# Row-block loading of W1 and six-bank accumulation for the first two token tiles of a fused attention and MLP kernel

## The chip, the cores and the metric

The kernel runs on one core of a Trainium2 chip. The metric is device time in microseconds of one execution. Before the change it took 204.91 us, the median of three runs (204.8 to 204.93).

A core has five engines that run beside each other: TensorE (PE in the profile; its weight loads are listed apart as PEld), VectorE (DVE), ScalarE (ACT), GpSimd (POOL) and SyncE (SP, which here only issues DMAs). They meet through semaphores. Every engine works through its own list of instructions in order, so an instruction that waits holds up everything behind it on that engine.

## The reference

```
x  = A_x                                   # 1 x 2048 x 640, bf16
xn = (x - mean(x)) / sqrt(var(x) + 1e-5)   # layer norm, no scale
A  = linear_attention(xn, wqkv) @ wo       # 32 heads, phi(t) = where(t > 0, t + 1, exp(t)) + 1e-6
B  = gelu(xn @ w1 + b1) @ w2 + b2          # w1: 640 x 1536, w2: 1536 x 640
out = x + A + B
```

Only the layer norm and the first half of B, `gelu(xn @ w1 + b1)`, are touched.

## The kernel before, in words

The 2048 tokens are 16 tiles of 128. For each tile the kernel loads x (`x_in`, tokens on the partitions), computes the layer norm (`xn_tm`) and turns the result over, so that features lie on the partitions (`xnT`, five blocks of 128 features: `DT` = 5). With xnT the MLP's hidden activations are computed as 12 units (`JT` = 12), each of 128 hidden features: five matmuls, one for each block k of features, with a 128x128 piece of W1 as the weight and xnT as the moving operand, summed in a PSUM bank, followed by a Gelu on ScalarE that writes `HG`. Later stages compute k, v, q, the attention sums and the output; they aren't changed.

The program is written through a small planner. `Pl.ins(engine, fn, reads, writes)` appends an instruction to the list of that engine and works out which semaphores it must wait for. Nothing is reordered: the order of the calls is the order on each engine. There are eight PSUM banks, taken in a ring by `take`.

The layer norm of a tile has four steps: `ln_half` (L335) twice, each a `bn_stats` on half of the features on VectorE, the first followed by a small GpSimd add that puts the epsilon in; `ln_aggr` (L343), a `bn_aggr` on VectorE and then a power of -0.5 on GpSimd that gives `rstd`; and `ln_norm` (L356) on VectorE. The turn to xnT has two forms. For tiles 0, 1 and 2 TensorE transposes into PSUM (`transp`, L362, `transp_part`, L399) and VectorE or ScalarE copies the result to xnT. For tile 3 and later SyncE issues a DMA transpose (`xnT_dma`, L453).

The opening, in the order of the calls:

- SyncE loads x tile 0, x tile 1, then W1 in pieces of 512 columns, with x tiles 2 and later between and behind them. ScalarE's queue issues b1 and the first two row blocks of the first 512 columns (`r_W1A`).
- TensorE runs matmuls on zeros (`filler`) until x arrives.
- Tile 0 is normalised and turned in two parts (`norm_part`, `transp_part`), and `h_first` (L408) computes units 0 to 3 of tile 0, then of tile 1, with 128 columns a matmul, in one bank for each unit.
- `units(0, 2, 4, 12)` computes the other eight units for both tiles together, 256 columns a matmul, with the transpose of tile 2 put between units 8 and 9.
- `units(2, 1, 0, 10)` and `units(3, 1, 0, 10)` follow for tiles 2 and 3 alone, then the last two units of both, then tiles 4 and 5, and so on.

On VectorE the statistics and norms of tiles 2 and 3 stand in the same list as the copies that TensorE's transposes feed, and the norm of each later tile follows in a loop.

Of the kernel before, what the change touches and what calls it, by code (L numbers as in the profile page):

```python
# [7 lines left out]
P = 128  # L8
# [104 lines left out]
def bass_parallel_sum__linear_attn_block__dense_activation_gelu__prompt_kernel(  # L113
# [24 lines left out]
    with contextlib.ExitStack() as es:  # L138
# [59 lines left out]
        def take(n):  # L198
            b = ring[0]
            if n == 2 and b % 2:  # L200
                b += 1
            b %= 8
            ring[0] = (b + n) % 8
            return b

        def bank(b, lo=0, hi=512):
            return ps[:, b * 512 + lo: b * 512 + hi]
# [9 lines left out]
        r_xb = [R_("xb%d" % t) for t in range(NT)]  # L217
        r_xn = [R_("xn%d" % t) for t in range(NT)]
        r_xnT = [R_("xnT%d" % t) for t in range(NT)]
        NW1 = 3  # L220
        r_W1A = R_("W1_0A")
        r_W1 = [R_("W1_%d" % i) for i in range(NW1)]
        r_Wq, r_Wk, r_Wv, r_W2 = R_("Wq"), R_("Wk"), R_("Wv"), R_("W2")
        r_Wo = [R_("Wo%d" % i) for i in range(2)]
        r_oT = [R_("oT%d" % i) for i in range(2 * DT)]
# [36 lines left out]
        def dma_w(eng, dst, src, res):  # L262
            Pl.ins(eng, lambda e: e.dma_start(dst, src), writes=[res], dma=True)  # L263

        w1v = B_w1.rearrange("(k p) n -> p k n", p=P)
        wqv = A_wqkv.rearrange("(k p) n -> p k n", p=P)
        FW = F // NW1
        def dma_w1(i, eng="sync"):
            dma_w(eng, W1[:, :, i * FW:(i + 1) * FW], w1v[:, :, i * FW:(i + 1) * FW], r_W1[i])
        KA = 2  # L270
        dma_x(0, 1)
        dma_w("scalar", b1tmp[:], B_b1.rearrange("(a p) -> a p", p=P), r_b1tmp)
        dma_w("scalar", W1[:, 0:KA, 0:FW], w1v[:, 0:KA, 0:FW], r_W1A)
        dma_x(1, 1)
        dma_w("sync", W1[:, KA:DT, 0:FW], w1v[:, KA:DT, 0:FW], r_W1[0])
        dma_w1(1)
        dma_x(2, 1)
        dma_w1(2)
        dma_x(3, 1)
        dma_x(4, 2)  # L280
        dma_x(6, 2)
# [40 lines left out]
        def filler(n):  # L322
            b = take(1)
            Pl.ins("tensor", [lambda e: e.matmul(bank(b), warm[:, 0:P], warm[:], start=True, stop=True)
                              for _ in range(n)], reads=[r_warm], writes=[B_[b]])
# [9 lines left out]
        def ln_half(t, h):  # L335
            s = t % 4
            Pl.ins(v, lambda e: e.bn_stats(stats[:, s, 6 * h:6 * h + 6], x_in[:, t, h * HW:(h + 1) * HW]),  # L337
                   reads=[r_x[t]], writes=[r_stats[s][h]])
            if h == 0:
                Pl.ins(g, lambda e: e.tensor_single_scalar(stats[:, s, 2:3], stats[:, s, 2:3], D * EPS, ALU.add),  # L340
                       reads=[r_stats[s][0]], writes=[r_stats[s][0]])

        def ln_aggr(t):  # L343
            s = t % 4
            Pl.ins(v, lambda e: e.bn_aggr(aggr[:, s, :], stats[:, s, :]),
                   reads=r_stats[s], writes=[r_aggr[s]])
            Pl.ins(g, lambda e: e.tensor_tensor(out=rstd[:, s:s + 1], in0=aggr[:, s, 1:2],
                                                in1=mhalf[:], op=ALU.pow),
                   reads=[r_aggr[s], r_small], writes=[r_rstd[s]])

        def ln_stats(t):
            ln_half(t, 0)
            ln_half(t, 1)
            ln_aggr(t)

        def ln_norm(t):  # L356
            s = t % 4
            Pl.ins(v, lambda e: e.tensor_scalar(xn_tm[:, t, :], x_in[:, t, :], aggr[:, s, 0:1], rstd[:, s:s + 1],  # L358
                                                ALU.subtract, ALU.mult),
                   reads=[r_x[t], r_aggr[s], r_rstd[s]], writes=[r_xn[t]])  # L360
# [16 lines left out]
        def h_unit(t0, n, jb):  # L377
            b = take(1)
            w = n * P
            tok = slice(t0 * P, t0 * P + w)  # L380
            Pl.ins("tensor", [(lambda e, k=k: e.matmul(  # L381
                bank(b, 0, w), W1[:, k, jb * P:(jb + 1) * P], xnT[:, k, tok],
                start=(k == 0), stop=(k == DT - 1))) for k in range(DT)],
                reads=[r_W1[jb * P // FW]] + r_xnT[t0:t0 + n], writes=[B_[b]])
            Pl.ins("scalar", lambda e: e.activation(  # L385
                HG[:, jb, tok], bank(b, 0, w), ACT.Gelu_apprx_tanh, bias=b1c[:, jb:jb + 1]),
                reads=[B_[b], r_b1c], writes=[r_HG[t][jb] for t in range(t0, t0 + n)])


        CA = 2 * P  # L390
        r_xnA, r_xnB = R_("xn0A"), R_("xn0B")

        def norm_part(t, lo, hi, res):
            s = t % 4
            Pl.ins(v, lambda e: e.tensor_scalar(xn_tm[:, t, lo:hi], x_in[:, t, lo:hi], aggr[:, s, 0:1], rstd[:, s:s + 1],
                                                ALU.subtract, ALU.mult),
                   reads=[r_x[t], r_aggr[s], r_rstd[s]], writes=[res, r_xn[t]])

        def transp_part(t, k0, k1, res):  # L399
            b = take(1)  # L400
            pT = bank(b).bitcast(BF16)
            Pl.ins("tensor", [(lambda e, k=k: e.transpose(pT[:, (k - k0) * P:(k - k0 + 1) * P],
                                                          xn_tm[:, t, k * P:(k + 1) * P], ident[:]))
                              for k in range(k0, k1)],
                   reads=[res, r_ident], writes=[B_[b]])
            return xnT[:, k0:k1, t * P:(t + 1) * P], pT[:, 0:(k1 - k0) * P].rearrange("p (k q) -> p k q", k=k1 - k0), b

        def h_first(t, jbs, resA, between=None):  # L408
            bs = [take(1) for _ in jbs]
            tok = slice(t * P, (t + 1) * P)  # L410
            for (ks, res) in (((0, 1), resA), ((2, 3, 4), r_xnT[t])):
                for i, (jb, b) in enumerate(zip(jbs, bs)):
                    Pl.ins("tensor", [(lambda e, k=k, jb=jb, b=b: e.matmul(
                        bank(b, 0, P), W1[:, k, jb * P:(jb + 1) * P], xnT[:, k, tok],
                        start=(k == 0), stop=(k == DT - 1))) for k in ks],
                        reads=[r_W1A if res is resA else r_W1[jb * P // FW], res], writes=[B_[b]])
                    if between and res is not resA and i in between:
                        between[i]()
            for jb, b in zip(jbs, bs):
                Pl.ins("scalar", lambda e, jb=jb, b=b: e.activation(  # L420
                    HG[:, jb, tok], bank(b, 0, P), ACT.Gelu_apprx_tanh, bias=b1c[:, jb:jb + 1]),
                    reads=[B_[b], r_b1c], writes=[r_HG[t][jb]])

        r_xnTA, r_xnTA1 = R_("xnT0A"), R_("xnT1A")
        r_xnA1, r_xnB1 = R_("xn1A"), R_("xn1B")
        Pl.ins("scalar", lambda e: e.activation(b1c[:, 0:1], warm[:, 0:1], ACT.Gelu_apprx_tanh),
               reads=[r_warm], writes=[r_b1c])
        filler(6)
        b1_step()
        filler(3)  # L430
        ln_stats(0)
        ln_half(1, 0)
        ln_half(1, 1)
        norm_part(0, 0, CA, r_xnA)
        norm_part(0, CA, D, r_xnB)
        ln_aggr(1)
        dA, sA, bA = transp_part(0, 0, 2, r_xnA)
        filler(1)
        dB, sB, bB = transp_part(0, 2, DT, r_xnB)
        Pl.ins("scalar", lambda e: e.activation(dA, sA, ACT.Copy), reads=[B_[bA]], writes=[r_xnTA])  # L440
        Pl.ins(v, lambda e: e.tensor_copy(dB, sB), reads=[B_[bB]], writes=[r_xnT[0]])
        norm_part(1, 0, CA, r_xnA1)
        norm_part(1, CA, D, r_xnB1)

        def copy_part(k0, k1, res, dst):
            d, s, b = transp_part(1, k0, k1, res)
            Pl.ins(v, lambda e: e.tensor_copy(d, s), reads=[B_[b]], writes=[dst])

        h_first(0, [0, 1, 2, 3], r_xnTA, {1: lambda: copy_part(0, 2, r_xnA1, r_xnTA1),
                                          3: lambda: copy_part(2, DT, r_xnB1, r_xnT[1])})  # L450
        h_first(1, [0, 1, 2, 3], r_xnTA1)

        def xnT_dma(t):  # L453
            Pl.ins("sync", lambda e: e.dma_start_transpose(xnT[:, :, t * P:(t + 1) * P], xn_tm[:, t, :]),
# [1 line left out]

        late = Pl.records["sync"][x_done:]
        del Pl.records["sync"][x_done:]
        JQ = JT // NW1

        def units(t0, n, lo, hi):
            for jb in range(lo, hi):
                h_unit(t0, n, jb)

        def ln_next(t):
            if t + 1 < NT:
                ln_half(t + 1, 0)
            ln_norm(t)
            if t + 1 < NT:
                ln_half(t + 1, 1)  # L470
                ln_aggr(t + 1)

        units(0, 2, JQ, 2 * JQ + 1)
        ln_stats(2)
        ln_norm(2)
        ln_stats(3)
        xnT_copy(2, transp(2))
        units(0, 2, 2 * JQ + 1, JT)
        ln_next(3)
        xnT_dma(3)  # L480
        units(2, 1, 0, 10)
        units(3, 1, 0, 10)
# [353 lines left out]
```

## Time and profile before

| | us |
|---|---|
| median of three runs | 204.91 |
| the profiled execution, own time | 205.15 |
| span of the profile | 203.5 |
| TensorE matmuls busy (share of the span) | 199.4 (98%) |
| VectorE busy | 122.1 (60%) |
| ScalarE busy | 73.6 (36%) |
| GpSimd busy | 14.4 (7%) |

The span runs from the first to the last instruction of the profiled execution; its own time is 1.65 us longer. All moments below are microseconds from the start of the span. Of the span's 1153 recorded matmuls, those on zeros count as busy too, so the busy share doesn't tell when the real work begins.

In the chain of work that ended last, every step is followed back to what released it; in the listing in order of time the columns are the start, the length and what ran. In the timeline the columns are start, length, engine, line, operation, output and inputs, shape, count, and in brackets the idle time of the engine before it with what ended it. In the table of windows the columns are the stretch, its length, the busy time (and count) of PE, PEld, DVE, ACT and POOL, the granted TensorE clock, the mean busy share of the 16 DMA engines and GB/s.

### The profile page before, as it was taken

The page shows a single profiled execution, that of the slowest core. Times are in us where ns is not written, and L with a number is a line of the kernel's source. Part 1 is how long each engine was busy: PE and PEld are TensorE (multiplying, and loading weights), DVE is VectorE, ACT ScalarE, POOL GpSimd, SP SyncE. Part 2 cuts the span into 40 slices and gives each one's busy share as a digit, 9 for nine tenths or more (in the row PEclk, how much of TensorE's full clock was granted, in tenths as well). Part 3 has the DMA queues.
Part 4 walks back from the last instruction along what each step waited for, and adds up shares of the span by engine and source line. Part 5 has one row for each costly group of instructions (what it writes and reads, how often), then busy time and mean ns, then how long its engine had stood idle before and what let it go on. Part 6 is the DMA issues. An engine that isn't in the chain of part 4 may idle for free.

```text
span 203.5 us, 3162 instructions
## 1 busy us (share of the span) xinstructions
PE 199.4 (98%) x1153; PEld 106.7 (52%) x1170; DVE 122.1 (60%) x246; ACT 73.6 (36%) x144; POOL 14.4 (7%) x43
## 2 busy tenths in 40 slices
PE   7999999999999999999999999999999999999996
PEld 2789885444444444644456565444444444444444
DVE  4579855000005899999458899595794297348222
ACT  3589886666667555121233596200000000000000
POOL 3136534000000000000000000000000000000000
PEclk9999999999999999999999999999999999999999
DMA  5974996999901111000179934117266926851541
GB/s 154 360 263 98 123 191 120 240 348 221 323 8 29 26 26 26 3 0 0 35 178 373 160 64 98 55 22 161 31 122 195 144 52 115 153 120 31 164 117 52
DMA packets 52550, 25.45 MB, mean 125 GB/s; under 512 B 38119, under 2 KB 52535, under 8 KB 52535
## 3 DMA queue, kind: packets, MB, share of 16 engines
q1 hardware_dynamic: 48782, 23.80, 50.1%
q10 hardware_dynamic: 3752, 1.45, 4.2%
q8 instruction: 9, 0.15, 0.3%
q14 instruction: 7, 0.05, 0.1%
HBM read 12.72 MB, written 2.62 MB: 75 GB/s over the span
## 4 chain that ended last, share of the span: by engine, by line
PE 90%; DMA 5%; DVE 2%; SPq 1%; issue 1%; POOL 0%; DVEq 0%
PE ps L745 29%; PE ps L381 21%; PE ps L584 11%; PE ps L573 8%; PE ps L532 8%; PE ps L710 7%; DMA xPK<-in_A_x_dram 3%; PE ps L563 2%; PE ps L523 2%; DMA xnT<-xn_tm 1%; DVE stats L337 1%; PE ps L598 1%; PE ps L616 1%; SPq L263 0%; DVE xn_tm L358 0%
## 5 line engine op out<-in xcount | busy, mean ns | idle before, releaser
L381 PE MATMUL ps<-xnT,W 128*128 128x256 bf16 (+2 forms) x372 | 50.5, 296 | 0.3
L385 ACT ACTIVATE HG<-ps,b1c 128x256 bf16<-128x256 f32 (+2 forms) x75 | 37.4, 522 | 13.5 <-PE ps L381 11.7
L745 PE MATMUL ps<-HG,W 128*128 128x512 bf16 x188 | 41.9, 379 | 0.2
L381 PEld LDWEIGHTS ps<-xnT,W 128*128 128x128 bf16 x375 | 32.2, 98 | 17.9 <-DMA xnT<-xn_tm 0.3
L745 PEld LDWEIGHTS ps<-HG,W 128*128 128x128 bf16 x192 | 18.8, 98 | 22.6
L584 PE MATMUL ps<-xnT,Wqkv 128*128 128x512 bf16 x97 | 22.4, 379 | 0.2
L745 PE MATMUL ps<-PQ,Msb 128*128 128x512 bf16 x78 | 17.8, 379 | 0.1
L532 PE MATMUL ps<-Wqkv,xnT 128*128 128x512 bf16 x78 | 17.8, 379 | 0.1
L573 PE MATMUL ps<-xPK,xn_tm 128*128 128x512 bf16 x78 | 17.2, 379 | 0.1
L337 DVE BATCH_NORM_STATS2 stats<-xPK 128x6 f32<-128x320 bf16 x32 | 13.7, 468 | 5.7 <-DMA xPK<-in_A_x_dram 5.7
L584 PEld LDWEIGHTS ps<-xnT,Wqkv 128*128 128x128 bf16 x100 | 11.3, 118 | 8.7
L507 ACT ACTIVATE xn_tm<-ps 128x512 bf16<-128x512 f32 x20 | 11.9, 597 | 9.5 <-PE ps L584 8.9
L510 DVE SCALAR_TENSOR_TENSOR PQ<-ps,xn_tm 128x512 bf16<-128x512 f32 x20 | 13.8, 692 | 2.1
L507 ACT ACTIVATE ek<-ps 128x512 bf16<-128x512 f32 x20 | 11.8, 597 | 8.4 <-PE ps L532 6.4
L518 DVE CAST b2c<-out_l 128x5 f32<-128x5 bf16 x1 | 0.2, 172 | 23.2 <-DMA out_l<-b2bc 23.2
L649 DVE TENSOR_REDUCE den_sb<-xn_tm 128x128 f32<-128x512 f32 x4 | 4.1, 1037 | 16.1 <-DMA xn_tm<-xn_tm 16.1
L751 DVE SCALAR_TENSOR_TENSOR W<-ps,b2c,xnT 128x512 bf16<-128x512 f32 x16 | 11.3, 734 | 2.8 <-PE ps L745 2.4
L532 PEld LDWEIGHTS ps<-Wqkv,xnT 128*128 128x128 bf16 x80 | 7.8, 98 | 9.4
L745 PEld LDWEIGHTS ps<-PQ,Msb 128*128 128x128 bf16 x80 | 7.8, 98 | 9.4
L573 PEld LDWEIGHTS ps<-xPK,xn_tm 128*128 128x128 bf16 x80 | 7.8, 98 | 9.3
L633 DVE SCALAR_TENSOR_TENSOR xn_tm<-PQ,z_sb,xn_tm 128x512 f32<-128x512 bf16 x16 | 12.0, 749 | 0.4
L510 DVE SCALAR_TENSOR_TENSOR xPK<-ps,ek 128x512 bf16<-128x512 f32 x16 | 11.1, 692 | 1.7
(66 smaller groups left out, 151.3 us busy)
## 6 DMA issues: line engine op xcount, KB each, us to landing
xPK<-in_A_x_dram SPq DMA_DIRECT2D x5, 640.0 KB, 6.9
Wqkv<-in_A_wqkv_dram SPq DMA_DIRECT2D x3, 800.0 KB, 7.6
W<-in_B_w_dram SPq DMA_DIRECT2D x1, 1920.0 KB, 15.0
out_dram<-xPK SPq DMA_DIRECT2D x3, 640.0 KB, 3.5
W<-in_B_w_dram SPq DMA_DIRECT2D x2, 640.0 KB, 7.7
xPK<-in_A_x_dram SPq DMA_DIRECT2D x4, 320.0 KB, 6.6
xn_tm<-xn_tm ACTq DMA_DIRECT2D x12, 64.0 KB, 3.2
Wo<-in_A_wo_dram SPq DMA_DIRECT2D x1, 750.0 KB, 12.6
```

Of the source, the lines that this page charges most:

```text
L337: Pl.ins(v, lambda e: e.bn_stats(stats[:, s, 6 * h:6 * h + 6], x_in[:, t, h * HW:(h + 1) * HW]), reads=[r_x[t]], writes=[r_stats[s][h]])
L381: Pl.ins("tensor", [(lambda e, k=k: e.matmul(bank(b, 0, w), W1[:, k, jb * P:(jb + 1) * P], xnT[:, k, tok], start=(k == 0), stop=(k == DT - ...
L385: Pl.ins("scalar", lambda e: e.activation(HG[:, jb, tok], bank(b, 0, w), ACT.Gelu_apprx_tanh, bias=b1c[:, jb:jb + 1]), reads=[B_[b], r_b1c ...
L507: Pl.ins("scalar", lambda e: e.activation(et, src, ACT.Exp), reads=[B_[b]], writes=[re])
L510: Pl.ins(v, lambda e: e.scalar_tensor_tensor(out=dst, in0=src, scalar=0.0, in1=et, op0=ALU.max, op1=ALU.add), reads=[B_[b], re], writes=[r ...
L532: Pl.ins("tensor", [(lambda e, k=k, b=b, t=t: e.matmul(bank(b), xnT[:, k, t * P:(t + 1) * P], Wqkv[:, k, D:D + CW], start=(k == 0), stop=( ...
L573: Pl.ins("tensor", lambda e, t=t, b=b, f=f: e.matmul(bank(b), xn_tm[:, t, f * P:(f + 1) * P], PK[:, t, 0:CW], start=(t == 0), stop=(t == N ...
L584: Pl.ins("tensor", [(lambda e, k=k, j=j, b=b: e.matmul(bank(b), Wqkv[:, k, j:D:DT], xnT[:, k, cc], start=(k == 0), stop=(k == DT - 1))) fo ...
L633: Pl.ins(v, lambda e: e.scalar_tensor_tensor(out=yv[c % 2], in0=pq, scalar=z_sb[:, j:j + 1], in1=yv[c % 2], op0=ALU.mult, op1=ALU.add), re ...
L710: return lambda e: e.matmul(bank(b, 0, cs.stop - cs.start), l, r[:, cs], start=(i == 0), stop=(i == JT + DT - 1))
L745: Pl.ins("tensor", lambda e, l=l, r=r, i=i: e.matmul(bank(b), l, r, start=(i == 0), stop=(i == JT + DT - 1)), reads=rd, writes=[B_[b]], ma ...
L751: Pl.ins(v, lambda e: e.scalar_tensor_tensor(out=oT[o], in0=bank(b), scalar=b2c[:, nb:nb + 1], in1=xnT[:, nb, cc], op0=ALU.add, op1=ALU.ad ...
```

## The change

W1 is loaded in five row blocks of 128 input features, all on SyncE's queue: block 0 after x tile 0, the others after x tile 1, and x tiles 2 and later after all of W1. Before, W1 came in column pieces on two queues.

Tiles 0 and 1 no longer use a bank for each unit. Two units share a bank of 512 columns: 128 columns for each of two tiles and two units. A matmul on zeros clears each of six banks, and every later matmul accumulates. For tile 0 the outer loop is now over k: `pass_k` issues the 12 matmuls of one row block. For tile 1, `bank_1` issues the ten matmuls that finish a bank, then two Gelus of 256 columns follow. Tile 0 is turned in three pieces (one, two and two blocks) and not two. The transpose of tile 2 stands before the last bank, and its copy on VectorE before the norm of tile 3.

The rstd of tile 0 is a reciprocal on VectorE and a square root on ScalarE; the other tiles keep GpSimd's power. ScalarE thus loads two tables of functions in the opening, first that of Sqrt, then that of Gelu, and issues the b1 load behind the first.

```diff
-        def dma_w1(i, eng="sync"):
-            dma_w(eng, W1[:, :, i * FW:(i + 1) * FW], w1v[:, :, i * FW:(i + 1) * FW], r_W1[i])
+        def dma_w1(k):
+            dma_w("sync", W1[:, k, :], w1v[:, k, :], r_W1[k])
         dma_x(0, 1)
-        dma_w("scalar", b1tmp[:], ...)
-        dma_w("scalar", W1[:, 0:KA, 0:FW], w1v[:, 0:KA, 0:FW], r_W1A)
+        dma_w1(0)
         dma_x(1, 1)
-        dma_w("sync", W1[:, KA:DT, 0:FW], w1v[:, KA:DT, 0:FW], r_W1[0])
-        dma_w1(1)
+        for k in range(1, DT):
+            dma_w1(k)
         dma_x(2, 1)
-        dma_w1(2)
...
+            if t == 0:
+                Pl.ins(v, lambda e: e.reciprocal(rstd[:, s:s + 1], aggr[:, s, 1:2]), ...)
+                Pl.ins("scalar", lambda e: e.activation(rstd[:, s:s + 1], rstd[:, s:s + 1], ACT.Sqrt), ...)
+                return
...
+        def pass_k(k, res, jbs):
+            for jb in jbs:
+                Pl.ins("tensor", lambda e, jb=jb: e.matmul(
+                    acc(jb, 0), W1[:, k, jb * P:(jb + 1) * P], xnT[:, k, 0:P],
+                    start=False, stop=False),
+                    reads=[r_W1[k], res], writes=[B_[jb // 2]])
+
+        def bank_1(i):
+            jbs = (2 * i, 2 * i + 1)
+            Pl.ins("tensor", [(lambda e, k=k, jb=jb: e.matmul(
+                acc(jb, 1), W1[:, k, jb * P:(jb + 1) * P], xnT[:, k, P:2 * P],
+                start=False, stop=(jb == jbs[-1] and k == DT - 1))) for jb in jbs for k in range(DT)],
+                reads=r_W1 + [r_xnT1A, r_xnT[1]], writes=[B_[i]])
+            for jb in jbs:
+                lo = (jb % 2) * 2 * P
+                Pl.ins("scalar", lambda e, jb=jb, lo=lo: e.activation(
+                    HG[:, jb, 0:2 * P], bank(i, lo, lo + 2 * P), ACT.Gelu_apprx_tanh, bias=b1c[:, jb:jb + 1]), ...)
...
-        filler(6)
-        b1_step()
-        filler(3)
+        Pl.ins("scalar", lambda e: e.activation(b1c[:, 0:1], warm[:, 0:1], ACT.Sqrt), ...)
+        dma_w("scalar", b1tmp[:], ...)
+        filler(3)
+        for i in range(NB):
+            Pl.ins("tensor", lambda e, i=i: e.matmul(bank(i), warm[:, 0:P], warm[:], start=True, stop=False), ...)
         ln_stats(0)
+        Pl.ins("scalar", lambda e: e.activation(b1c[:, 1:2], warm[:, 0:1], ACT.Gelu_apprx_tanh), ...)
+        for i, (k0, k1) in enumerate(pieces):        # (0, 1), (1, 3), (3, 5)
+            norm_part(0, k0 * P, k1 * P, ...)
+        turn_0(0)
+        turn_0(1)
+        ln_stats(1)
+        norm_part(1, 0, D, [r_xn[1]])
+        pass_k(0, kres[0], range(4))
+        turn_0(2)
+        pass_k(0, kres[0], range(4, JT))
+        pass_k(1, kres[1], range(JT))
+        ring[0] = 7
         b1_step()
+        for k in range(2, 4):
+            pass_k(k, kres[k], range(JT))
+        transp_part(1, 0, 2, r_xn[1], 6)
+        copy_part(1, 0, 2, 6, v, r_xnT1A)
+        transp_part(1, 2, DT, r_xn[1], 7)
+        copy_part(1, 2, DT, 7, "scalar", r_xnT[1])
+        pass_k(4, kres[4], range(JT))
+        ln_half(2, 0); ln_half(2, 1); ln_aggr(2)
+        ln_half(3, 0); ln_half(3, 1); ln_norm(2); ln_aggr(3)
+        for i in range(NB):
+            bank_1(i)
+            if i == NB - 2:
+                ring[0] = 7
+                xnT_copy(2, transp(2))
+        ring[0] = NB
...
+        ln_half(4, 0)
+        ln_norm(3)
+        ln_half(4, 1)
+        ln_aggr(4)
         xnT_dma(3)
         units(2, 1, 0, 10)
         units(3, 1, 0, 10)
```

The removed calls of `h_first`, `units(0, 2, ...)` and `ln_next` are left out here.

## The prediction

> **What bounds the kernel now.** I read the engine shares and the chain on the page first, then the chain in order of time, then the timeline of the first 22 us, then one-microsecond windows.
>
> ```profile
> PE 199.4 (98%) x1153; PEld 106.7 (52%) x1170; DVE 122.1 (60%) x246; ACT 73.6 (36%) x144; POOL 14.4 (7%) x43
> PE 90%; DMA 5%; DVE 2%; SPq 1%; issue 1%; POOL 0%; DVEq 0%
> ```
>
> TensorE bounds the kernel, so a change to the opening is worth only what it moves the moment from which TensorE runs without a break. The chain in order of time gives that moment.
>
> ```profile
> 2.73 7.05 DMA xPK<-in_A_x_dram
> 9.80 0.90 DVE stats L337 x2
> ...
> 13.68 0.41 DVE stats L337
> 14.09 0.44 DVE xn_tm L358
> 14.56 2.66 DMA xnT<-xn_tm
> 17.27 13.92 PE ps L381 x150
> ```
>
> The load of x tile 2 (landing 9.78) holds VectorE; VectorE's order holds the normalisation of tile 3 until 14.09; its DMA transpose lands at 17.22; from 17.27 TensorE runs to the end. Call that moment T3: the first matmul of tile 3's units. The timeline shows the rest of the opening.
>
> ```profile
> 4.41 0.57 POOL L347 TENSOR_TENSOR rstd<-aggr,mhalf 128x1 f32<-128x1 f32 x1 [0.48 <-DVE aggr L345]
> 5.08 0.76 DVE L395 TENSOR_SCALAR xn_tm<-xPK,aggr,rstd 128x256 bf16<-128x256 bf16 x2
> 6.45 1.22 PE L413 MATMUL ps<-xnT,W 128*128 128x128 bf16 x14
> 11.70 0.44 PEld L381 LDWEIGHTS ps<-xnT,W 128*128 128x128 bf16 x5 [0.22 <-DMA W<-in_B_w_dram]
> 12.26 0.45 PE L365 MATMUL ps<-ident,xn_tm 128*128 128x128 bf16 x5
> 17.27 4.76 PEld L381 LDWEIGHTS ps<-xnT,W 128*128 128x128 bf16 x69 [0.30 <-DMA xnT<-xn_tm]
> ```
>
> Real matmuls start at 6.45; the last W1 piece costs 0.22; before T3 TensorE waits only 0.30. So two paths end almost together at T3, and lengthening either by more than 0.3 moves the end. After T3 one landing is nearly as tight: tile 7's transpose lands at 26.02 (trace), TensorE takes it at 26.08. Why it is late is in the DMA share:
>
> ```profile
> 21.00:22.00 1.00, 1.00 (x11) 0.90 (x10) 0.57 (x2) 0.85 (x3) 0.39 (x2) 1.00 0.54 107
> 22.00:23.00 1.00, 1.00 (x11) 0.90 (x10) 1.00 (x4) 0.86 (x2) 0.64 (x2) 1.00 2.21 69
> 23.00:24.00 1.00, 1.00 (x11) 0.89 (x10) 0.99 (x5) 0.93 (x2) 0.44 (x2) 1.00 0.27 44
> ```
>
> The last two columns are DMA share and GB/s. A share of 2.21 with 69 GB/s is packets that stand still. The packet records show a 16 KB instruction packet at 21.50 (1.46 us), transpose packets of 256 B stuck from 22.14 to 23.7, and another at 35.74 with transpose packets stuck from 35.81 to 37.4. Both times the DMA transposes stop until 1.7 to 2.2 us after the fetch began.
>
> **What the Trainium skill says.** "Runtime: NRT & Kernel Launch", section Instruction fetch mechanics: instructions come in 16 KiB blocks of 256. This trace: nine such packets for some 2,323 TensorE records, which fits; that they stop transposes is the trace's, not the page's. "ScalarE: Activation LUTs", What ACT_TABLE_LOAD costs: 1283 ns and a drain of 1380 ns. The trace has 1.283 (1.95, and before the first Exp) but the next ACTIVATE starts 12 ns after it, so I use 1.28. "TensorE: Matmul & The Clock Gate", Part 1: the array runs at half rate until an activity window of 3.4 us was busy. The trace agrees on the rates: 128-column matmuls 107 ns apart until 6.73, 56 ns after; the window's threshold isn't seen. "DMA: Bandwidth & Descriptors", Why small descriptors are slow: a fixed cost for each packet. The trace: 46 ns for 1024 B, 55 for 1280 B.
>
> **The change part by part** (us from the span's start).
>
> *Rstd of tile 0.* Removed: GpSimd's pow, 4.41 to 4.97, and the way back to 5.08. Added: a reciprocal of 128x1. The nearest rows are the aggregate on 12 elements (0.21) and the reciprocal of 128 elements (0.95); I take 0.17, bounds 0.1 to 0.5. Then a Sqrt, like the 128x1 ACTIVATE (0.20). With gaps of 0.04 to 0.07 between engines the first norm starts at 4.32+0.04+0.17+0.05+0.20+0.06 = 4.84: 0.24 earlier. The Sqrt table loads while x is still on its way; the b1 DMA now waits behind it on ScalarE (from 0.80 to about 2.3), hidden, as b1 is needed near 8. The Gelu table then loads after the Sqrt, 4.77 to 6.06, and the two ScalarE copies of xnT queue behind it: piece 1 at 6.2 to 6.58, needed near 7.1. Hidden; without cover it would cost that 1.3.
>
> *Fillers and zeroing.* Ten fillers become three and six matmuls that zero banks: 9 x 0.427 = 3.84, 1.25 to 5.09, under the wait for tile 0. Cost nothing.
>
> *First pieces.* Norms of 128, 256, 256 columns (256 takes 0.35; 128 about 0.30): first ends 5.14, transpose 5.2 to 5.5, VectorE copy after the third norm, 5.6 to 5.83, first real matmul 0.14 later (as 6.30 to 6.44 before): 5.97, against 6.44. The array is still at half rate until 6.73: about 0.3 lost.
>
> *Matmuls of tiles 0 and 1.* Before 80 of 128 columns; now 120, for 40 fewer of 256 columns: 80 x 0.056 against 40 x 0.109, +0.1. TensorE's order up to the start of tile 1's sums: five passes of 12 (3.36), two, one and five transposes (0.45), 0.3 of half rate: the last pass could start at 5.97+4x0.67+0.45+0.3 = 9.4.
>
> *W1 in row blocks.* Each is 384 KB, 8 packets of 3072 B an engine. From 46 and 55 ns a packet should take about 118 (an estimate): 0.94 a block; at the old rate per byte 1.10. Data flows from about 3.0. Five blocks and x tile 1 (0.44) end at 8.2 to 8.9 on a quick engine. But engines differ: the last old W1 piece landed from 9.60 to 11.65 over its 16 engines. With that 2.0 the last block lands between 8.2 and 10.9; I take 9.8. It costs 0.4. x tile 2, now behind all W1, lands 10.25; its stats and norm then end near 12.6, before TensorE asks for them at 13.3: hidden by 0.7.
>
> *Tile 3's path.* Tile 1's sums start 9.8+0.05+0.67 = 10.5; their inputs, two copies behind the transposes of tile 1, are there about then too. Five banks of ten matmuls take 2.8: 13.3. Only now comes tile 2's transpose, and VectorE is in order: copy of tile 2 waits for it, and behind the copy stand ln_half(4,0) and the norm of tile 3. Transposes 0.45 and 0.06 to the copy, 0.36 to the stats, 0.41 to the norm, 0.45 norm, 0.03, 2.66 landing, 0.05: 4.47. T3 = 17.77, +0.5. TensorE itself would be there at 13.3+0.56+0.2+2.8 = 16.9.
>
> *ScalarE.* Twelve Gelus of 256 columns replace eight of each width. Spacing back to back is 0.25 at 128 columns (9.37, 9.62, 9.87), plus (0.473-0.367) = 0.36. A bank needs 0.71 against 0.56 of matmuls; over six banks it falls 0.9 behind, but bank 5 is reused only by the eighth later unit, 2.2 later. Hidden.
>
> *What is late next.* 39 more matmuls and transposes net mean 78 more TensorE instructions (a weight load each), so the block fetched at 21.50 before is asked for some 1.6 after T3, near 19.4, instead of 4.2 after. In flight then is tile 5's transpose (issue T3+0.5, landing T3+3.1). Stopped until 21.05 to 21.6, with nearly all its 1.2 still to move, it lands 22.3 to 22.9. TensorE needs it at T3+3.9 = 21.7. I take a stall of 0.7; bounds 0 (the fetch falls elsewhere) and 1.5.
>
> Sum: +0.5+0.7 = +1.2. The profiled execution took 205.15 (span 203.5 and 1.65 around it), so it would be 206.35; against the median of 204.91 I forecast 206.1.
>
> **The rivals.** *No collision*: T3 moves 0.1 to 0.6 and nothing else: 205.3. For: the place of the fetch rests on two events. Against: both stopped transposes. *Late opening*: TensorE's activity from 3.3 to 6.7 falls from about 88% to 79% busy, as it idles around 5.1 to 5.97; if the half rate then lasts another 3.4 us window, the passes cost 107 ns a matmul, tile 1's sums start near 12.1 and T3 is 19.2: +1.9; W1 rows landing at 11.2 give the same. 206.8, or 207.6 with the collision. *Faster*: VectorE and TensorE reach tile 3 sooner. T3 = first matmul + 11.2 if neither W1 nor the clock costs anything; T3 gains only when the first matmul is before 6.05. With 5.97 and no half rate the gain is 0.1; it needs 5.6 for 0.4: 204.5. The price lies in the 4.47 after bank 4. *Nothing changes*, the tight paths shifting together, is within the second case.
>
> **How the numbers follow.** Collision 0.42, none 0.27, late opening 0.20, faster 0.11. A measurement of this kernel tells about 0.2% (0.41 us). Slower: 0.42+0.20 and somewhat under half of 0.27 = 0.74; same 0.15; faster 0.11. The range 204.9 to 207.7 leaves out the faster case, the lower edge of no collision, and the worst of late opening; the likeliest case alone spans 205.5 to 206.8.
>
> **What would show it.** Right: first real matmul near 6.0, last pass waiting for W1 near 9.8, tile 2's transposes near 13.3, T3 near 17.8, a wait for xnT near 21.7 with a DMA share over 1. Wrong: W1's last row before 9.3; 107 ns spacing past 7; a T3 before 17.3; no wait after T3.

## The result and the profile after

The changed kernel takes 206.5 us, the median of four runs (206.34 to 207.16), against 204.86 for the kernel before, run beside it (204.71 to 204.93). The ratio is 1.0087 with an interval of 1.0064 to 1.0111: slower, by four times the 0.2% that a measurement here can tell. One version below, the one with x tiles 2 and 3 ahead of W1, has two of its four executions at a granted clock of 0.984 and 0.992 instead of 1.00, and only its other two are compared. The profiled execution took 206.36 with a span of 204.8; for the kernel before these were 205.15 and 203.5. So by the two profiled executions the change costs 1.2 to 1.3, by the medians 1.64.

The page of the changed kernel, engine shares and chain, in the same columns as before:

```profile
PE 199.7 (98%) x1192; PEld 107.5 (52%) x1209; DVE 122.1 (60%) x246; ACT 74.4 (36%) x145; POOL 13.7 (7%) x42
PE 92%; DMA 4%; SPq 1%; issue 1%; DVE 1%
```

TensorE still sets the end, and its recorded busy time grew by only 0.3. The cost is in waits of the opening, so the chain in order of time is the next view (start, length, what ran):

```profile
3.14 6.03 DMA W<-in_B_w_dram
...
9.21 0.84 PE ps L424 x12
...
11.11 2.85 PE ps L431 x50
13.96 0.29 PE ps L365 x5
...
14.28 0.04 DVE xnT L373
...
14.69 0.48 DVE stats L332
15.17 0.35 DVE xn_tm L358
...
15.54 2.66 DMA xnT<-xn_tm
...
18.25 4.06 PE ps L381 x60
22.31 0.19 issue
22.50 9.55 PE ps L381 x86
```

Read it from the top. The chain no longer begins with an x tile but with W1: its row blocks release the passes of tile 0. Then come the ten-matmul sums of tile 1 (L431), the transposes of tile 2 between them (L365), VectorE's copy, the statistics and norm that stand behind that copy, and tile 3's DMA transpose. T3 is 18.25, against 17.27 before: +0.98. After it the chain breaks once more, at 22.31, and the units of tiles 4 and 5 from block 2 on start at 22.50 instead of 21.16: +1.34. (Before, the line at 17.27 in the prediction runs through that place: 69 weight loads without a wait.) The span grew by 1.30, so what was lost was lost before 22.5. One thing changed later: the wait for tile 7 near 26.1, which delayed the matmuls by 0.04 before, is gone, and 1.34 less 0.04 is the 1.30.

The timeline of the changed kernel has the waits on that chain (start, length, engine, line, what, count, idle before and its releaser):

```profile
4.35 0.16 DVE L343 RECIPROCAL rstd<-aggr 128x1 f32<-128x1 f32 x1
4.55 0.20 ACT L344 ACTIVATE rstd<-rstd 128x1 f32<-128x1 f32 x1 [2.26 <-DVE rstd L343]
5.89 0.59 PE L424 MATMUL ps<-xnT,W 128*128 128x128 bf16 x4
7.14 0.67 PEld L424 LDWEIGHTS ps<-xnT,W 128*128 128x128 bf16 x12 [0.23 <-DMA W<-in_B_w_dram]
...
9.21 0.67 PEld L424 LDWEIGHTS ps<-xnT,W 128*128 128x128 bf16 x12 [0.28 <-DMA W<-in_B_w_dram]
14.28 0.49 DVE L373 COPY xnT<-ps 128x640 bf16<-128x640 bf16 x1 [1.06 <-PE ps L365]
18.24 3.78 PEld L381 LDWEIGHTS ps<-xnT,W 128*128 128x128 bf16 x60 [0.63 <-DMA xnT<-xn_tm]
22.47 1.55 PEld L381 LDWEIGHTS ps<-xnT,W 128*128 128x128 bf16 x15 [0.45 <-issue]
```

Three things are to be seen. The first real matmul runs at 5.89, 0.55 earlier than before, but the passes of tile 0 then stop for W1 again and again. VectorE stands idle for 1.06 at 14.28 until TensorE gives it tile 2's transposes, while tile 3's norm waits behind that copy; then TensorE in turn waits 0.63 for tile 3, against 0.30 before. And at 22.47 it waits for the transposes of tiles 4 and 5. The last wait is marked "issue", so its cause has to be read elsewhere. The windows (stretch, length, busy time of the five engines, granted clock, DMA share, GB/s):

```profile
20.00:21.00 1.00, 1.00 (x22) 1.00 (x20) 0.99 (x5) 1.00 (x5) 0.71 (x2) 1.00 1.97 128
22.00:23.00 1.00, 0.81 (x8) 0.51 (x7) 0.57 (x2) 0.74 (x2) 0.37 (x2) 1.00 0.39 78
```

A DMA share of 1.97 at 128 GB/s is again packets that stand still. The packet records place a 16 KB instruction packet at 19.56 (1.31 us), and transpose packets stuck from 20.46 to 21.67. Tile 4's transpose, issued at 17.46, lands at 21.91, tile 5's at 22.41. TensorE could have used them at 22.14 (50 matmuls 0.056 apart and ten 0.109 apart after T3) and starts at 22.50: a wait of 0.36.

That these blocks are TensorE's can be counted. In the traces of all twelve kernels this block is asked for after 218 to 226 recorded weight loads of TensorE, whether that is at 15.5 or at 27.5.

### The profile page after: what moved, and what is told of

Read it like the earlier page. It is cut to its first block, busy times and chain, and to the rows that moved or that the text cites. A ratio compares the mean times of both kernels' runs of the same rounds, so it can differ in the third digit from the quotient of the medians.

```text
span 204.8 us, 3245 instructions
## 1 busy us (share of the span) xinstructions
PE 199.7 (98%) x1192; PEld 107.5 (52%) x1209; DVE 122.1 (60%) x246; ACT 74.4 (36%) x145; POOL 13.7 (7%) x42
## 4 chain that ended last, share of the span: by engine, by line
PE 92%; DMA 4%; SPq 1%; issue 1%; DVE 1%
PE ps L768 29%; PE ps L381 21%; PE ps L607 11%; PE ps L596 8%; PE ps L555 8%; PE ps L733 7%; DMA W<-in_B_w_dram 3%; PE ps L586 2%; PE ps L546 2%; PE ps L431 1%; DMA xnT<-xn_tm 1%; PE ps L424 1%; PE ps L621 1%; PE ps L639 1%; SPq L262 1%
## 5 line engine op out<-in xcount | busy, mean ns | idle before, releaser
L381 PE MATMUL ps<-xnT,W 128*128 128x512 bf16 (+2 forms) x332 | 46.0, 299 | 0.8 <-DMA xnT<-xn_tm 0.5
L385 ACT ACTIVATE HG<-ps,b1c 128x512 bf16<-128x512 f32 (+2 forms) x67 | 33.6, 546 | 12.7 <-PE ps L381 11.4
L381 PEld LDWEIGHTS ps<-xnT,W 128*128 128x128 bf16 x335 | 28.5, 98 | 18.1 <-DMA xnT<-xn_tm 0.6
L574 DVE TENSOR_TENSOR Msb<-Msb,xPK 128x640 f32<-128x640 f32 x14 | 11.6, 826 | 0.5
```

The costliest lines, as they stand in the source:

```text
L381: Pl.ins("tensor", [(lambda e, k=k: e.matmul(bank(b, 0, w), W1[:, k, jb * P:(jb + 1) * P], xnT[:, k, tok], start=(k == 0), stop=(k == DT - ...
L385: Pl.ins("scalar", lambda e: e.activation(HG[:, jb, tok], bank(b, 0, w), ACT.Gelu_apprx_tanh, bias=b1c[:, jb:jb + 1]), reads=[B_[b], r_b1c ...
```

## The experiments

**The theory** after the traces: the cost is a sum of a later T3 (+0.98) and a fetch of instructions that stops the transposes of tiles 4 and 5 (+0.36). In the first part, the pace at which W1's row blocks land and the order of the work around tile 2's transposes each have a share. **The rivals:** x tile 2, loaded behind all of W1, is what holds T3; the new rstd of tile 0 costs or gains something; the wait after T3 isn't the fetch but only T3's own shift. Below, T3 and the start of the units of tiles 4 and 5 from block 2 on (18.25 and 22.50 in the changed kernel, 17.27 and 21.16 before) are the two marks that each trace is read by. A wait of TensorE at the second mark or later is given as the delay of its matmuls beyond their spacing; the bracket in a line of weight loads is their idle time and up to 0.1 longer. Versions that differ by half a microsecond have intervals that overlap, so it is the marks that decide between them.

### W1's pace taken away

```diff
-  acc(jb, 0), W1[:, k, jb * P:(jb + 1) * P], ...   reads=[r_W1[k], res]
+  acc(jb, 0), W1[:, 0, jb * P:(jb + 1) * P], ...   reads=[r_W1[0], res]
```

The same in the sums of tile 1. Row blocks 1 to 4 of W1 are still loaded, but tiles 0 and 1 leave them out and use block 0 in all five steps, so nothing waits for them.

> The changed kernel, but all hidden units of tiles 0 and 1 multiply with W1's row block 0 in all five steps and wait for that block alone (so these two tiles' activations are not the reference's; every load, matmul and copy stays). Theory 'W1 paces TensorE' : passes 1 to 4 no longer wait (7.14, 8.26, 9.21, 10.26 in the changed kernel), tile 1's sums start near 9.8 instead of 11.0, tile 2's transposes come as soon as its norm is done (near 13.1), and T3, the first matmul of tile 3's units, moves from 18.25 to 17.6: about 0.6 us faster than the changed kernel, 205.9. Rival 'x tile 2 behind W1 holds VectorE': its load still lands near 10.7, T3 stays within 0.2 of 18.25 and the time at 206.5. Rival 'shared banks and Gelus': no change either.

Measured: 206.02 (205.76 to 206.46), ratio 1.0062 (1.0037 to 1.0087). The timeline, TensorE's weight loads:

```profile
9.96 2.81 PEld L431 LDWEIGHTS ps<-xnT,W 128*128 128x128 bf16 x50
13.43 0.28 PEld L365 LDWEIGHTS ps<-ident,xn_tm 128*128 128x128 bf16 x5 [0.67 <-DVE xn_tm L358]
17.90 3.78 PEld L381 LDWEIGHTS ps<-xnT,W 128*128 128x128 bf16 x60 [0.56 <-DMA xnT<-xn_tm]
```

The sums of tile 1 start at 9.96 instead of 11.00. Most of that is what W1's pace costs them; about 0.3 is that the array was at full rate by 5.13 in this execution and only from 6.47 in that of the changed kernel. But T3 moves by only 0.35, because the wait moves on: TensorE now stops at 13.43 for tile 2's norm, whose x tile landed at 10.94, behind W1. So W1's pace is the first limit, and x tile 2 stands 0.35 behind it here; with the landing of the changed kernel (10.66) it would be about 0.6, an estimate.

### x tiles 2 and 3 ahead of W1

```diff
-  for k in range(1, DT):
-      dma_w1(k)
   dma_x(2, 1)
   dma_x(3, 1)
+  for k in range(1, DT):
+      dma_w1(k)
```

> The changed kernel with x tiles 2 and 3 loaded before W1's row blocks 1 to 4. Theory 'W1 paces TensorE': every later row block lands 0.9 later, the last near 11.1, tile 1's sums start near 11.8 and T3 goes from 18.25 to about 19.1: 0.9 us slower than the changed kernel, 207.4. Rival 'x tile 2 behind W1 holds VectorE': x tile 2 lands near 5.6, statistics of tiles 2 and 3 come earlier and T3 falls to 17.6 or less, 205.9 or less.

Measured: 206.91, which is the profiled execution, and 207.54 (the median of all four is 208.48, 206.91 to 210.04, and the ratio 1.0206, 1.0158 to 1.0253). Timeline:

```profile
9.82 0.67 PEld L424 LDWEIGHTS ps<-xnT,W 128*128 128x128 bf16 x12 [0.82 <-DMA W<-in_B_w_dram]
18.86 3.78 PEld L381 LDWEIGHTS ps<-xnT,W 128*128 128x128 bf16 x60 [0.63 <-DMA xnT<-xn_tm]
```

x tile 2 now lands at 5.57, five microseconds early, and T3 is 0.6 later: the rows of W1 land later (the last at 10.80 instead of 10.22), the waits for them reach 0.82, and tile 1's sums start at 11.6. That is some two thirds of the forecast, in which the rows were 0.9 later. The rival that x tile 2 holds T3 in the changed kernel falls; W1's rows hold it, by a run in each direction.

### The order around tile 2

```diff
-            if i == NB - 2:
+            if i == NB - 3:
                 ring[0] = 7
                 xnT_copy(2, transp(2))
 ...
-        ln_half(4, 0)
         ln_norm(3)
+        ln_half(4, 0)
```

Tile 2's transposes come one bank earlier, and tile 3's norm is no longer behind half of tile 4's statistics.

> The changed kernel with two orders altered: the transposes of tile 2 stand one bank earlier on TensorE, and the norm of tile 3 stands ahead of the first statistics of tile 4 on VectorE. Theory 'VectorE's order behind the late transposes holds tile 3': transposes at 13.2, norm of tile 3 near 14.1 to 14.5, its landing near 17.2, and then TensorE itself is last, at 17.7: T3 17.7 against 18.25, about 0.5 us faster than the changed kernel, 206.0. Rival 'the load queue or the DMA transpose itself is last': T3 stays at 18.2, 206.5.

Measured: 205.91 (205.39 to 206.56), ratio 1.0057 (1.0035 to 1.0078). Timeline:

```profile
14.76 6.61 PEld L381 LDWEIGHTS ps<-xnT,W 128*128 128x128 bf16 x110
21.93 2.09 PEld L381 LDWEIGHTS ps<-xnT,W 128*128 128x128 bf16 x20 [0.57 <-DMA xnT<-xn_tm]
```

The unbroken run of 110 weight loads is the reading: it covers the 100 matmuls of tiles 2 and 3, T3 at 17.60 included, with no wait between. The DMA transpose of tile 3 is issued at 14.77 and lands at 17.43, before TensorE asks. So of the +0.98 at T3, 0.65 was this order: VectorE standing still for tile 2's transposes while tile 3's norm waited behind. The other 0.33 is TensorE itself, whose sums of tile 1 start at 11.19 here, behind W1's last row (10.37). The two alterations were not run apart. Part of the gain goes again at 21.93: with an earlier T3 but a fetch that moved only by 0.3 (19.27; packets stuck from 20.09 to 21.05) the wait for tile 5 grows from 0.36 to 0.48. At the second mark (21.97) 0.53 of 0.65 is left.

### Tile 0's rstd as before

```diff
-  if t == 0:
-      ... reciprocal on VectorE, Sqrt on ScalarE ...
-      return
-  ... activation(b1c[:, 0:1], warm[:, 0:1], ACT.Sqrt)
+  ... activation(b1c[:, 0:1], warm[:, 0:1], ACT.Gelu_apprx_tanh)
```

GpSimd's power gives rstd for tile 0 too, and only one table is loaded.

> The changed kernel with tile 0's rstd by GpSimd's power again and only the Gelu table loaded. The first real matmul goes from 5.89 to about 6.15. Theory 'W1 paces TensorE': pass 0 still ends near 7.15, when row block 1 lands (7.09), so T3 and the time stay within 0.2 us of the changed kernel, 206.5. Rival 'the reciprocal and Sqrt are worth their 0.24': 0.2 to 0.3 us slower, 206.8. If the Sqrt's second table load cost anything, it would be faster.

Measured: 206.47 (206.14 to 207.07), ratio 1.0085 (1.0059 to 1.0111), the same as the changed kernel. Timeline:

```profile
6.11 0.24 PEld L419 LDWEIGHTS ps<-xnT,W 128*128 128x128 bf16 x4 [0.32 <-issue]
18.24 3.78 PEld L376 LDWEIGHTS ps<-xnT,W 128*128 128x128 bf16 x60 [0.64 <-DMA xnT<-xn_tm]
```

The first real matmul comes 0.25 later (6.14 against 5.89), and T3 is the same 18.25: the next pass waits for W1 either way. The rstd edit gains what it promises in its place and is worth nothing.

### The fetch moved by narrow matmuls

TensorE's instructions come in blocks, so more of them early on bring each later fetch forward. Narrow matmuls on zeros, with 32 columns in the weight and in the moving operand, are about 27 ns apart and do that at little cost of time. First in the changed kernel, 30 of them for the three wide fillers:

```diff
-        filler(3)
+        filler(0, 30)   # 30 matmuls of 32x32 on zeros
```

> The changed kernel with its three wide matmuls on zeros replaced by 30 narrow ones (32 x 32), 54 more TensorE instructions in the opening with nothing else changed. Theory 'the instruction fetch stops the transposes': the fetch at 19.56 comes about 27 matmuls (1.5 us) earlier, near 18.1, between the landings of tiles 3 and 4; tile 4 lands near 21.0 and tile 5 before 22.1, so the 0.36 us wait after T3 goes: 206.1. Rival 'the transposes of tiles 4 and 5 are late because their norms are late': the wait stays at 0.36, 206.5. In both, T3 stays near 18.25 as W1 still paces the passes.

Measured: 206.76 (206.48 to 208.29), ratio 1.01 (1.0073 to 1.0127): not faster. The timeline at the second mark:

```profile
22.64 8.42 PEld L383 LDWEIGHTS ps<-xnT,W 128*128 128x128 bf16 x78 [0.59 <-issue]
```

The fetch moved as meant, to 18.25, and its stuck packets to 19.17 to 20.31, so tile 4 landed at 21.00 instead of 21.91. But tile 5's transpose, next in SyncE's list, was issued only at 19.94 and landed at 22.58, and the wait grew from 0.36 to 0.50. Moving the fetch by 1.3 us isn't enough: the stop only hits an earlier transpose, and that one pushes the next.

The same thing from the other side, in the kernel before, 42 narrow matmuls for three of the wide ones, which is 78 more TensorE instructions, as many as the change brought:

```diff
-        filler(6)
+        filler(3, 42)
```

> As the earlier trial on the kernel before, with 78 more TensorE instructions in the opening, but with seven of the ten wide matmuls on zeros kept (42 narrow ones replace three), so that TensorE stays busy until tile 0 is ready and the half-rate stretch stays as in the kernel before. Theory 'the instruction fetch stops the transposes': T3 17.3, fetch near 19, tile 5 lands near 21.5 and TensorE waits 0.3 to 0.5 at 21.16; tile 7 is no longer stopped by that fetch: 205.2 to 205.4. Rival 'the narrow matmuls cost time through the clock alone': no wait at 21.16, and the time as before, 204.85.

Measured: 205.1 (204.34 to 205.83), ratio 1.0001 (0.9987 to 1.0016): no difference that can be told. T3 stays at 17.27. The windows and the timeline of this run:

```profile
19.00:20.00 1.00, 1.00 (x22) 1.00 (x20) 0.99 (x5) 1.00 (x5) 0.70 (x2) 1.00 1.51 131
```

```profile
21.25 9.84 PEld L383 LDWEIGHTS ps<-xnT,W 128*128 128x128 bf16 x91 [0.20 <-issue]
```

The share over 1 is now two to three microseconds earlier than in the kernel before (22 to 23). The fetch is at 18.56. Tile 4's and tile 5's transposes are issued at 16.48 and 17.80 as before, but tile 4 lands at 20.64 instead of 19.06 and tile 5 at 21.19 instead of 20.37, and a wait of 0.11 appears at 21.28 where there was none. So the instructions alone do make the wait, and a later T3 or later norms have no part in it here. (Full rate came earlier than before, by 5.6, but T3 is the same.) The size is less than forecast, 0.11 for 0.3 to 0.5. Tile 7's transpose, which the old fetch had helped to hold until 26.02, now lands at 24.50, and the 0.04 that it delayed the matmuls is gone; the span is 0.07 longer, which the times can't tell. Tile 7 still takes 3.85 from issue to landing, where tile 3 takes 2.67: two 8 KB instruction packets of another queue and the next x load fall into that stretch, and no run separates these. A fetch costs what it hits, and in the versions run here it hit one transpose or another.

An earlier try replaced six wide fillers and one more by 46 narrow ones:

```diff
-        filler(6)
+        filler(0, 46)
 ...
-        filler(3)
+        filler(2)
```

> The kernel before with ten wide matmuls on zeros replaced by 46 narrow and three wide ones, 78 more TensorE instructions, as many as the change adds, and nothing else changed. Theory 'the instruction fetch stops the transposes': the fetch at 21.50 comes 39 matmuls earlier, near 19.0, tile 5's transpose (landing 20.37 before) lands 21.5 to 22.3 and TensorE, which wants it at 21.16, waits 0.3 to 1.1 us: 205.2 to 206.0. Rival 'no such effect': the time stays at 204.9. T3 is 17.27 in both, if the narrow matmuls end before tile 0 is ready.

Measured: 205.98 (205.53 to 207.03), ratio 1.0058 (1.0039 to 1.0076). It showed a wait of 0.32 for tile 5 at 21.6 behind a fetch at 18.92, but also something that spoils it: the narrow ones were done early, TensorE stood idle from 3.8 to 5.5, and full rate came only at 8.22 instead of 6.73. Its time can't be given to the fetch alone; the version above keeps seven wide fillers for that reason.

Last, the best order with the fetches moved out of the transposes, by some 75 narrow matmuls put where TensorE waits:

```diff
-        filler(3)
+        filler(0, 48)
 ...
+        narrow(7, 8)   # after tile 0's first transpose; 6, 8, 8 more ahead of pass 1, after it and after pass 2
```

> The changed kernel with the two altered orders of the earlier trial, and in addition about 75 more narrow matmuls on zeros, put where TensorE waits for tile 0 and for W1 (150 instructions). The fetch that fell at 19.27 comes about 75 matmuls earlier, near 14.8, before tile 3's transpose moves data. Theory 'the instruction fetch stops the transposes': tiles 4 and 5 land near 19.7 and 21.0, the 0.48 wait at 21.96 goes: 205.4, still slower than before. The fetch before it moves into the loads of W1 and may cost up to 0.3 there. Rival 'those transposes are late by VectorE's order': the wait stays, 205.9.

Measured: 205.92 (205.3 to 206.59), ratio 1.0041 (1.003 to 1.0052). Timeline:

```profile
18.41 8.69 PEld L387 LDWEIGHTS ps<-xnT,W 128*128 128x128 bf16 x105 [0.19 <-DMA xnT<-xn_tm]
27.30 3.73 PEld L387 LDWEIGHTS ps<-xnT,W 128*128 128x128 bf16 x35 [0.20 <-issue]
```

No fetch falls between 15.52 and 23.19, tile 5 lands at 21.59, and TensorE runs through the place where it waited. T3 is later here, which would hide a late landing, so tile 5 has to be counted from T3: TensorE asks for it 3.89 after T3; it landed 4.16 after T3 in the changed kernel and 4.28 with the order alone, and 3.18 here, as in the kernel before (3.10). So the wait after T3 is the fetch's.

The gain is lost in other places; the forecast was 205.4. T3 is 18.41, 0.8 later than with the order alone. Of that 0.6 is the start of tile 1's sums (11.81 for 11.19), as W1's last row lands at 10.94 instead of 10.37. The fetch at 11.76 comes after that landing and can't be its cause; what is, no trace shows. The other 0.2 is tile 3's transpose: the fetch at 15.52 falls on it, and it takes 2.97 instead of 2.66. The fetch at 11.76 lies in the loads of x, and x tiles 4 and 5 land at 14.15 instead of 12.17. The fetch at 23.19 holds tile 7's transpose, which delays the matmuls by 0.11 near 27.3.

### The row blocks alone

```diff
-  W1 in pieces of 512 columns, the first of them in two parts
+  W1[:, k, :] for k in 0..4, in the places of the change; every unit waits for the rows it uses
```

The kernel before, with nothing changed but the loads of W1 and what the matmuls wait for.

> The kernel before with only the W1 loads changed to five row blocks on SyncE's queue (block 0 after x tile 0, the rest after x tile 1, x tiles 2 and 3 behind W1); the matmuls keep their order by units. Theory 'W1's last row block comes near 10.2 whatever waits for it': units 0 to 3 wait for it from about 7.3, then 40 x 0.056 less what is done, eight units of 0.55, transposes and 2.8 for tile 2 follow, T3 near 19.5: about 2.2 us slower than before, 207.1. So the block-by-block sums would recover about half of what the row blocks cost. Rival 'the row loads themselves are faster and cost nothing': at most 0.5 slower.

Measured: 210.73 (210.16 to 211.3), ratio 1.0274 (1.0244 to 1.0304). The timeline and the windows of this run:

```profile
11.06 0.80 PE L413 MATMUL ps<-xnT,W 128*128 128x128 bf16 x6 [2.32 <-DMA W<-in_B_w_dram]
14.96 3.93 PE L381 MATMUL ps<-xnT,W 128*128 128x256 bf16 x25
```

```profile
8.00:11.00 3.00, 0.74 (x7) 0.47 (x5) 0.62 (x2) 0.00 (x0) 0.00 (x0) 1.00 1.03 395
14.00:17.00 3.00, 3.00 (x21) 2.40 (x20) 1.88 (x6) 1.80 (x5) 1.00 (x4) 1.00 0.04 16
20.00:23.00 3.00, 3.00 (x51) 2.93 (x49) 2.89 (x10) 2.85 (x10) 1.53 (x4) 1.00 0.27 55
```

T3 is 23.43. Tile 0's norm stands behind x tile 1's statistics on VectorE, and x tile 1 now lands at 5.24 behind a whole row block, so the first real matmul is at 7.73 instead of 6.44. A unit that sums over all of k can't end before the last row of W1 (10.81), so TensorE then stands from 8.5 to 11.06: that was expected. What wasn't is the third thing. From 14 to 17 TensorE is 100% busy with the granted clock at 1.00, as it is from 20 to 23, and yet it executes 21 matmuls in one stretch and 51 in the other. The shapes differ (about half of the 21 have 256 columns, of the 51 only eight), but that isn't all. The matmul records show the rate: 256 columns are 0.213 apart until 17.08 and 0.109 apart from then on, and 128 columns 0.107 and 0.056, so the array is at half rate from its first real matmul to 17.08. The kernel before had reached full rate at 6.73. Here TensorE is idle from 5.5 to 6.45 and again from 8.5 to 11.06, and that these two gaps are the reason is argued, not tested. The work from 11.06 to 17.08 takes 6.0 where full rate takes 3.0, so half rate is some 3 us of the 6.1 by which this execution is longer. By the medians the rows alone cost 5.9, and the rest of the change wins back 4.2: its sums go on block by block and keep TensorE at work through the loads, at full rate from 6.47.

### x tile 3 earlier in the kernel before

```diff
-  dma_w1(2)
+  dma_w("sync", W1[:, :, 2 * FW:2 * FW + FH], ...)
   dma_x(3, 1)
+  dma_w("sync", W1[:, :, 2 * FW + FH:F], ...)
```

> The kernel before with the last column piece of W1 loaded in two halves and x tile 3 between them. x tile 3 lands near 11.2 instead of 12.10, the last half of W1 near 12.1, before its units ask for it at 12.7. The 0.22 wait at 11.70 goes. Theory 'T3 is the later of two paths': the statistics of tile 3 still stand behind the norm of tile 2 (12.2), so its path stays near 17.2 while TensorE is ready at 16.8: same as before, 204.9 (gain 0 to 0.2). Rival 'x tile 3's landing sets T3': 0.5 faster, 204.4.

Measured: 204.88 (204.25 to 207.11), ratio 1.0007 (0.9992 to 1.0021): the same. T3 is 17.19, 0.08 earlier, and TensorE's matmuls are held there by 0.13 instead of 0.29. The span is 0.12 shorter, too little for the times to show. The kernel before has next to nothing to gain at T3 on either path: an earlier tile 3 could win another 0.13 at most before TensorE itself is last.

No version that was run is faster than the kernel before.

## Why the prediction was right

It gave 206.1 for a measured 206.5, and its range and its likeliest case, a later T3 and a collision with a fetch, are what the traces show. Its sum was +1.2 against the profiled execution, which gives 206.35; that execution took 206.36. The mechanism was right; that the sum comes out to 0.01 is luck. Two terms were mis-sized, +0.98 for +0.5 at T3 and +0.36 for +0.7 after it, and their errors cancelled.

- **Rstd of tile 0.** The reciprocal took 0.16 (0.17 predicted), the first norm started at 4.79 (4.84), the first real matmul at 5.89 (5.97). "Hidden" held for the Gelu table and the two copies behind it (6.17, 6.67). That the earlier start is worth nothing is shown by the run without it.
- **The clock.** "About 0.3 lost" to half rate was high: matmuls were 56 ns apart from 6.47. The rival in which half rate lasts another 3.4 us did not happen. It was worth naming: with the row blocks alone half rate lasts to 17.08.
- **W1 in row blocks.** A packet of 3072 B took 121 ns (118 estimated). The last block landed at 10.22, inside the range of 8.2 to 10.9 but 0.42 after the value taken; the copies of tile 1 cost another 0.1, and tile 1's sums started at 11.00 instead of 10.5. The count "before 80 of 128 columns" is a slip, as the kernel before has 40 of 128 and 40 of 256; the sum behind it (80 more of 128 against 40 fewer of 256, +0.1) is right. This is the first mis-sized term: the last pass, which the prediction's order of work allowed at 9.4, started at 10.26.
- **x tile 2 hidden by 0.7.** In the changed kernel its norm ended at 13.10 and its transposes began at 13.74, so 0.64 was left. But it does stand next in line: with W1's wait gone it took over.
- **Tile 3's path.** From tile 2's transposes to T3 4.47 were predicted and 4.5 measured, with the same steps. T3 was 18.25 for 17.77: +0.98 for +0.5, and the difference is W1's. TensorE would itself have been there at about 17.6, not 16.9: of the 0.7 between, some 0.4 is W1's, and 0.28 is tile 2's five transposes, which the sum had left out. In the run with the other order it is last, at 17.60.
- **ScalarE.** Twelve Gelus, 0.36 apart as worked out, and no bank waited for them.
- **What is late next.** The fetch came at 19.56 (19.4 predicted), tile 5 landed at 22.41 (22.3 to 22.9). The stall was 0.36 and not 0.7: the second mis-sized term. The prediction put the fetch 1.6 after T3, and it came 1.32 after. Counted back in the trace of the kernel before, 39 weight loads ahead of the one at 21.50 is 1.36 to 1.41 after T3; so the 1.6 was some 0.2 too much, and only T3, later by 0.48, brought the fetch near 19.4. From T3 the fetch was thus earlier than predicted and tile 5 with it, and TensorE asked at 22.14 instead of 21.7.

The row of rivals stands thus: "no collision" is refuted by the wait at 22.47 and by the run that removes it; "late opening" is right in that W1's last row was late, but far from its 11.2; "faster" needed the first matmul at 5.6 and got 5.89, and the passes behind it waited for W1 anyway.

What stays open: the medians differ by 0.4 more than the profiled executions do. The profiled execution of the kernel before (205.15) lies 0.3 above its median and that of the changed kernel (206.36) 0.1 below its own. That is within the scatter: four executions of the kernel before happened to lie within 0.2, but 35 of them, run beside later versions, go from 204.31 to 205.76. The traces account for +1.30 of the span; for what the medians have beyond it there is no cause on record. No version undoes the late T3 and the fetch together without a loss elsewhere.

## What to carry to other kernels

Cutting a weight by rows of the contraction lets the first sums start early, but each of them then ends with the last row: ask when the last block lands on the slowest DMA engine, and whether the work behind it, above all another engine's in-order list, was placed for the earlier moment. When two paths meet at one point with 0.3 of slack, an early start on the path that is last is worth at most that slack and on the other nothing, and a delay is paid in full, on the other as far as it goes beyond the slack. And where DMA transposes feed TensorE just in time, count its instructions: where a fetch falls among them decided a few tenths of a microsecond here, and moving it chose which transfer it stopped.

## What the runs showed of the hardware

- A fetch of a 16 KB block of TensorE's instructions does more than hold the packets in flight: the next DMA transpose in SyncE's list is issued late too (tile 5's at 19.94, behind packets stuck from 19.17 to 20.31, in the first run with narrow matmuls). In each of the twelve traces the transposes in flight at such a fetch stood still until 1.7 to 2.3 after it began (21.50 to 23.76 in the kernel before, 27.45 to 29.28 with the row blocks alone).
- With the row blocks alone the array needed 6.0 us of unbroken work, from 11.06 to 17.08, to reach full rate, while the granted clock of the profile read 1.00 all along. "TensorE: Matmul & The Clock Gate" of the Trainium skill, Part 1, says that the window of 3.4 us runs freely and doesn't start with the work. That fits: work that begins within a window has to last through the next one as well, so up to 6.8, an estimate from the page's figure. The window's own edges are not in the trace. The start of full rate does shift between executions whose TensorE work opens alike: it was there by 5.13 in the run with W1's pace taken away, and only at 6.47 in the changed kernel.
- The 16 DMA engines end one load far apart in the opening: W1's last row block was in on the first at 9.12 and on the last at 10.22, and it is the last that releases.
